# Pooled attention and a top-2 mixture of experts on one core: the unrolled expert part holds 1200 rows per expert instead of 1216

## The chip, the core and the metric

The kernel runs on one core of a Trainium2 chip. A core has TensorE (PE in the profile, with its weight loads as PEld), VectorE (DVE), ScalarE (ACT), GpSimd (POOL) and SyncE (SP). They share an on-chip memory (SBUF), and PE writes its products into PSUM, which DVE and ACT read. The metric is the device time of one execution in microseconds (us); lower is better.

## What is computed

Attention with keys and values averaged over eight positions gives 4608 token rows `x` of 512. A noisy gate then sends each row to the two best of eight experts. Each expert is a two-layer product, and the rows come back weighted:

```python
top2 = np.argpartition(-noisy_logits, 2, axis=1)[:, :2]
top2_w = np.exp(top2_l - top2_l.max(-1, keepdims=True)); top2_w /= top2_w.sum(-1, keepdims=True) + 1e-09
for e in range(E):                       # E = 8, x: 4608 x 512, w1[e]: 512 x 1024, w2[e]: 1024 x 512
    for k in range(2):
        mask = top2[:, k] == e
        h = np.maximum(x[mask] @ w1[e], 0.0)
        out[mask] += top2_w[mask, k, None] * (h @ w2[e])
```

On average an expert gets 4608 x 2 / 8 = 1152 rows. The reference evaluated on its inputs gives the eight experts 1135, 1130, 1185, 1163, 1193, 1176, 1107 and 1127 rows. In the kernel the list of expert 0 has two gaps (its second half begins at row 512 at the earliest, and a later part at row 896), so that it ends at row 1174.

## The kernel before

The first part (to about 184 us of the trace) is attention: products, exponentials, and at its end the gate. Each token's two (row, weight) records are scattered into `rec_dram`, a list for each expert with room for `ER` rows. The list is filled ahead with an index out of range (`BIG`), so that unused places are gathered from a harmless row and never written.

The second part is the experts, one after the other, unrolled. The first `CAP` = 1216 places of each list are cut into tiles of 128 places, `t` = 0 to 9, of which tile 9 has 64. The tiles form three groups: tiles 0 to 3 (512 columns), tiles 4 to 6 (384) and tiles 7 to 9 (128 + 128 + 64 = 320). Expert 0 takes them in the order (0-3), (4-6), (7-9), the other seven in the order (0-3), (7-9), (4-6). For each group:

- `gather` (L703) fetches rows of `x` by indirect DMAs, four for a tile (two for tile 9). They are issued by POOL, and so are all other indirect DMAs.
- `split` (L917) turns each tile by a DVE transpose (`xt`) and cuts it into a high part `xh` (ACT, L939) and a low part `xl` (DVE, L939).
- `stage1` (L956) makes the first product in eight blocks `f` of 128 hidden columns. A block is 12 matmuls (four depth blocks, and the three products high-high, low-high, high-low) into a PSUM tile `ph`, of which there are three. ACT takes the block out as `hh` (L973) and DVE as `hl` (L974). Every second block (every block for tiles 0-3) a piece of later weights is converted too (L484, L485). Its staging buffers `wst` are refilled by SP.
- `stage2` (L1023) makes the second product. For tiles 0-3 and 4-6 it takes 24 matmuls of 512 columns for each tile into a PSUM tile `py` (three buffers). `finish` (L1003) multiplies by the token's weight, adds what `out` held (`pv`, gathered by POOL at L992) and scatters it (L1014).
- For tiles 7-9 the second product is turned the other way: four PSUM tiles `py` (`mb` = 0 to 3), each 24 matmuls with the tokens as columns (L1043). DVE transposes each into `yt` (L1048). Ten slices of 32 tokens are then multiplied and added (L1054) to what ten gathers (L1031) brought into the buffer `pv4`, and scattered (L1057). Tile 3 uses the same buffer `pv4` for its own rows, so the ten gathers wait until the scatter of tile 3 has landed.

After the eight experts a loop (L1210) takes any further rows, 128 at a time. Its count is worked out on the chip from `CAP`, and each turn loads its expert's weights anew.

A scheduler orders the instructions of each engine when the program is built. Each engine works through its own list in order, and waits between engines are semaphores that the tile framework sets. The framework takes two accesses to one PSUM bank as dependent even where they touch different columns.

Of the kernel before, what the change touches and what calls it, by code (L numbers as in the profile page):

```python
# [20 lines left out]
def kernel(  # L21
# [12 lines left out]
    nc = tc.nc  # L34
# [4 lines left out]
    P = 128  # L39
# [8 lines left out]
    NCH = 9  # L48
    EARLY = 4 * P
    EARLY2 = 7 * P  # L50
    SECT = ((0, 4, P), (4, 3, P), (7, 2, P), (9, 1, 64))
    CAP = 1216
    OV_T = -(-(NTOK - CAP) // P)
    ER = CAP + OV_T * P
    XT0 = NTOK // 2
    BIG = float(1 << 20)
# [574 lines left out]
    def load_recs(e0, e1, s0, s1, early=False):  # L631
        ne = e1 - e0
        t0, t1 = SECT[s0][0], SECT[s1 - 1][0] + SECT[s1 - 1][1]
        nt = t1 - t0
        nm = f"{e0}_{e1}_{t0}"
        V = nc.vector
        raw = rp.tile([P, ne, nt, 2], I32, name=f"raw{nm}")
        if s1 == len(SECT):
            V.memset(raw[64:, :, nt - 1, 0:1], int(BIG))
            V.memset(raw[64:, :, nt - 1, 1:2], 0)  # L640
        src = rec_dram.rearrange("(e r) c -> e (r c)", e=E)
        for ts, n, np_ in SECT[s0:s1]:
            o = ts * P * 2
            with nullcontext() if early else tc.issue_after(wld[1, 1, 0]):
                ld = (nc.gpsimd if RE >> (0 if early else 1 if e0 == 0 else 2) & 1 else nc.sync).dma_start(raw[:np_, :, ts - t0:ts - t0 + n].rearrange("p e t c -> p e (t c)"),
                                   src[e0:e1, o:o + np_ * n * 2].rearrange("e (p x) -> p e x", p=np_))
            genl[0] = ld.ins
            if early:
                tc.add_to_no_dep_group("rec_load0", ld.ins)

        def tl(w, dt=F32):
            return rp.tile([P, ne, nt], dt, name=f"{w}{nm}")

        w = ne * nt

        def spread(src, nm_):
            px = mone(f"{nm_}{nm}")
            for r in range(4):
                nc.tensor.matmul(px[:, r * w:(r + 1) * w], sel[:, r].rearrange("p u j -> p (u j)"),
                                 src.rearrange("p e t -> p (e t)"), start=True, stop=True)  # L660
            return px[:, :4 * w].rearrange("p (r e t) -> p r e t", r=4, e=ne)

        def late():
            xf = tl("xf")
            nc.gpsimd.tensor_copy(xf, raw[:, :, :, 0])
            wf = tl("wf")
            nc.gpsimd.tensor_copy(wf, raw.bitcast(F32)[:, :, :, 1])
            o = rp.tile([P, 4, ne, nt], I32, name=f"o{nm}")
            V.tensor_scalar(o, spread(xf, "px"), 4.0, qcol, op0=OP.mult, op1=OP.add)
            w4 = rp.tile([P, 4, ne, 3], F32, name=f"w4{nm}")  # L670
            V.tensor_copy(w4, spread(wf, "pw")[:, :, :, 7 - t0:10 - t0])
            x = rp.tile([P, 4, ne, nt], I32, name=f"x{nm}")
            V.tensor_single_scalar(x, o, float(4 * NTOK - 1), op=OP.min)
            for e in range(E):
                for t in range(7, 10):
                    oi4[e, t] = o[:, :, e, t:t + 1]
                    wc4[e, t] = w4[:, :, e, t - 7:t - 6]
                if e:
                    for t in range(10):
                        xi[e, t] = x[:, :, e, t:t + 1]  # L680

        if e1 == 1:
            x = tl("x", I32)
            nc.gpsimd.tensor_single_scalar(x, raw[:, :, :, 0], float((XT0 if t1 <= 4 else NTOK) - 1), op=OP.min)
        else:
            x = rp.tile([P, 3], I32, name=f"x{nm}_0")
            nc.gpsimd.tensor_single_scalar(x, raw[:, 0, 7:10, 0], float(NTOK - 1), op=OP.min)
            for t in range(7, 10):
                xi[0, t] = x[:, t - 7:t - 6]
        for e in range(0 if e1 == 1 else 1, e1):  # L690
            for t in range(t0, t1):
                i = (e - e0, t - t0)
                if e1 == 1:
                    xi[e, t] = x[:, i[0], i[1]:i[1] + 1]
                tokc[e, t] = raw[:, i[0], i[1], 0:1]
                wcol[e, t] = raw.bitcast(F32)[:, i[0], i[1], 1:2]
        return late
# [105 lines left out]
    for b in range(2, B):  # L803
        c = 9 * ((b - 2) // 2) + (0 if b % 2 == 0 else 4)
# [7 lines left out]
    for b in range(1, B):  # L812
        c = 9 * (b // 2) + (0 if b % 2 == 0 else 4)
# [96 lines left out]
    def w2s(e, hl, f):  # L910
        return W[e, 2 + f // 4][:, hl, (f % 4) * DM:(f % 4 + 1) * DM]
# [39 lines left out]
    pv4 = mp.tile([P, 10, P], F32, name="pv4")  # L951

    def cols(grp):
        return 320 if grp[1] == 7 else grp[2] * P

    def stage1(grp, hook=None):  # L956
        e, t0, nt = grp
# [65 lines left out]
    def stage2(grp, mid, hook=None):  # L1023
        e, t0, nt = grp
        hs = HT.pop(grp)
        n = cols(grp)
        if t0 == 7:
            yt = mp.tile([P, 10, NDB, 32], F32, tag="yt", name=f"yt{e}")
            if e:
                for i in range(10):  # L1030
                    g = nc.gpsimd.indirect_dma_start(  # L1031
                        out=pv4[:, i], out_offset=None, in_=out4,
                        in_offset=bass.IndirectOffsetOnAxis(ap=oi4[e, t0 + i // 4][:, i % 4], axis=0),
                        bounds_check=4 * NTOK - 1, oob_is_err=False)
                    tc.declare_no_dep(g.ins, group=f"out{e}", reason="rows of other tokens")
                    tc.add_to_no_dep_group(f"out{e}", g.ins)
            mid()
            for mb in range(NDB):
                py = mps.tile([P, DM], F32, tag="py", name=f"py{e}_{t0}_{mb}", bufs=3)
                i = 0  # L1040
                for f in range(NFB):
                    for a, b in PASSES:
                        nc.tensor.matmul(  # L1043
                            py[:, :n],
                            w2s(e, b, f)[:, mb * P:(mb + 1) * P],
                            hs[f][a][:, :n], start=(i == 0), stop=(i == 3 * NFB - 1))
                        i += 1
                nc.vector.transpose(yt[:, :, mb], py[:, :n].rearrange("p (c j) -> p c j", j=32))  # L1048
            r4 = pv4
            for i in range(10):  # L1050
                y = yt[:, i].rearrange("p m j -> p (m j)")
                wc = wc4[e, t0 + i // 4][:, i % 4]
                if e:
                    nc.vector.scalar_tensor_tensor(r4[:, i], y, wc, pv4[:, i], op0=OP.mult, op1=OP.add)  # L1054
                else:
                    nc.vector.tensor_scalar(r4[:, i], y, wc, None, op0=OP.mult)
                s = nc.gpsimd.indirect_dma_start(  # L1057
                    out=out4, out_offset=bass.IndirectOffsetOnAxis(ap=oi4[e, t0 + i // 4][:, i % 4], axis=0),
                    in_=r4[:, i], in_offset=None, bounds_check=4 * NTOK - 1, oob_is_err=False)
                for gr in (f"out{e}", f"outb{e}"):  # L1060
                    tc.declare_no_dep(s.ins, group=gr, reason="rows of other tokens")
                tc.add_to_no_dep_group(f"out{e}", s.ins)
            return
        pvs = [prev(e, t, P) for t in range(t0, t0 + nt)]
        mid()
        for t in range(t0, t0 + nt):
            cs = slice((t - t0) * P, (t - t0 + 1) * P)
            py = mps.tile([P, DM], F32, tag="py", name=f"py{e}_{t}", bufs=3)
            i = 0
            for f in range(NFB):  # L1070
                for a, b in PASSES:
                    lastm[0] = nc.tensor.matmul(py, hs[f][a][:, cs], w2s(e, b, f),  # L1072
                                                start=(i == 0), stop=(i == 3 * NFB - 1))
                    i += 1
            finish(e, t, P, py, pvs.pop(0))
            if hook:
                hook(t - t0)

    def mone(name):
        return mps.tile([P, 512], F32, tag="xp", name=name, bufs=2)  # L1080
# [63 lines left out]
    for i, g in enumerate(groups):  # L1144
# [18 lines left out]
        if i == 0:  # L1163
            lates.append(load_recs(0, E, 0, 4))
            fetch(groups[2])
            with tc.issue_after(hli[g, NFB - 1].ins):
# [3 lines left out]
    thr = rp.tile([P, OV_T], F32, name="thr")  # L1170
    nc.gpsimd.iota(thr, pattern=[[P, OV_T]], base=CAP, channel_multiplier=0,
                   allow_small_or_imprecise_dtypes=True)
# [19 lines left out]
    nc.vector.tensor_sub(sg[:, 1:2], prow, red[:, 1:2])  # L1192
    nc.vector.tensor_scalar(sg[:, 0:1], red[:, 0:1], float(ER), float(CAP), op0=OP.mult, op1=OP.add)
    nc.vector.scalar_tensor_tensor(sg[:, 0:1], sg[:, 1:2], float(P), sg[:, 0:1], op0=OP.mult, op1=OP.add)
# [15 lines left out]
    with tc.For_i(0, totr, 1) as it:  # L1210
# [34 lines left out]
        py = ops.tile([P, DM], F32, name="opy")  # L1245
# [35 lines left out]
```

## Time and profile before

| | us |
|---|---|
| median of 3 runs | 1040.61 |
| range of the runs | 1039.6 to 1043.3 |
| the profiled execution, its own time | 1040.2 |
| its span, first to last instruction | 1038.1 |
| PE busy | 1015.6 |
| POOL busy | 636.0 |
| DVE busy | 561.3 |
| ACT busy | 339.5 |

The span is 2.1 us shorter than the time of the execution, which also covers what lies around the first and the last instruction. Busy times are sums over a span with two different parts, so a stage is read from its own stretch of the trace. In a row of the trace the bracket gives how long the engine stood idle before the instruction and what released it. A matmul's duration in a row covers its whole way through the array; matmuls overlap, so how fast they follow each other is read from their starts or from the length of a stage.

### The profile page before, as it was taken

What the parts mean: (1) busy time and instruction counts of PE and PEld (TensorE: products, weight loads), DVE (VectorE), ACT (ScalarE), POOL (GpSimd) and SP (SyncE); (2) the same over time, 40 slices, a digit from 0 to 9 for tenths busy, and PEclk for the clock granted to TensorE, in tenths of its full rate; (3) what the DMA queues carried; (4) which work ended last, traced back from release to release, by engine and by line L of the source; (5) the groups of instructions that cost most, each with busy time, mean ns of one, the idle gap of its engine ahead of it and who ended that gap; (6) DMA issues with size and microseconds to landing.
All of it is one profiled execution on the core that took longest, in us unless ns stands there. A gap on an engine that the chain in (4) does not pass through costs nothing. (4 is left out here: it accounts for less than half of the span.)

```text
span 1038.1 us, 16083 instructions
## 1 busy us (share of the span) xinstructions
PE 1015.6 (98%) x5896; PEld 917.2 (88%) x5896; DVE 561.3 (54%) x1289; ACT 339.5 (33%) x857; POOL 636.0 (61%) x662
## 2 busy tenths in 40 slices
PE   7999999999999989999999999999999999999996
PEld 6999898889988988899889988998899889988995
DVE  6799897923654545454545454446444644554331
ACT  5588788402321232123212221222222222222110
POOL 4004555565777677767767775777577757773541
PEclk9799999999999999999999999999999999999999
DMA  9997985754333423442444234424342443232200
GB/s 322 363 339 243 241 272 185 183 157 124 102 93 116 135 67 114 131 132 69 124 126 140 69 115 128 135 70 120 118 130 75 117 122 120 80 91 87 69 20 31
DMA packets 77028, 142.13 MB, mean 137 GB/s; under 512 B 24501, under 2 KB 32778, under 8 KB 76948
## 3 DMA queue, kind: packets, MB, share of 16 engines
q1 hardware_dynamic: 48628, 78.33, 24.7%
q0 software_dynamic: 28320, 62.77, 20.2%
q8 instruction: 47, 0.77, 0.3%
q14 instruction: 33, 0.27, 0.1%
HBM read 103.78 MB, written 39.17 MB: 138 GB/s over the span
## 5 line engine op out<-in xcount | busy, mean ns | idle before, releaser
L968 PE MATMUL ph<-xh,w 128*128 128x384 f32 (+2 forms) x1536 | 404.3, 344 | 3.4 <-DVE hl L974 2.7
L714 POOL DMA_INDIRECT xg<-x_dram,x x266 | 260.6, 980 | 91.5 <-issue 66.1
L968 PEld LDWEIGHTS ph<-xh,w 128*128 128x128 f32 x1536 | 274.5, 188 | 24.1 <-DVE hl L974 3.0
L973 ACT ACTIVATE hh<-ph 128x512 fp32r<-128x512 f32 (+2 forms) x192 | 97.8, 509 | 552.2 <-PE ph L968 552.2
L1072 PE MATMUL py<-w,hh 128*128 128x512 f32 x896 | 276.5, 390 | 0.0
L968 PE MATMUL ph<-xl,w 128*128 128x320 f32 (+2 forms) x768 | 263.8, 344 | 0.0
L974 DVE SCALAR_TENSOR_TENSOR hl<-ph,hh 128x512 fp32r<-128x512 f32 (+2 forms) x192 | 111.1, 579 | 218.5 <-ACT hh L973 218.4
L1072 PEld LDWEIGHTS py<-w,hh 128*128 128x128 f32 x896 | 167.8, 188 | 34.2
L1072 PE MATMUL py<-w,hl 128*128 128x512 f32 x448 | 174.5, 390 | 0.0
L968 PEld LDWEIGHTS ph<-xl,w 128*128 128x128 f32 x768 | 144.2, 188 | 10.2
L1010 DVE SCALAR_TENSOR_TENSOR pv<-py,raw,pv 128x128 f32<-128x128 f32 x196 | 54.9, 342 | 130.9 <-PE py L1072 122.7
L1043 PE MATMUL py<-hh,w 128*128 128x320 f32 x512 | 112.8, 309 | 0.0
L1057 POOL DMA_INDIRECT out_dram<-pv,o x80 | 83.7, 1046 | 36.1 <-issue 14.3
L1072 PEld LDWEIGHTS py<-w,hl 128*128 128x128 f32 x448 | 84.1, 188 | 17.5
L1031 POOL DMA_INDIRECT pv<-out_dram,o x70 | 73.7, 1053 | 39.4 <-DMA out_dram<-pv,raw 20.2
L614 POOL DMA_INDIRECT rec_dram<-rec,pos x72 | 75.7, 1051 | 29.2 <-issue 19.8
L1014 POOL DMA_INDIRECT out_dram<-pv,raw x56 | 58.6, 1047 | 51.1 <-DVE pv L1010 31.7
L485 DVE TENSOR_TENSOR w<-wst,w 128x512 fp32r<-128x512 f32 x128 | 87.4, 686 | 0.9 <-ACT w L484 0.5
L1043 PEld LDWEIGHTS py<-hh,w 128*128 128x128 f32 x512 | 85.6, 188 | 0.0
L1043 PE MATMUL py<-hl,w 128*128 128x320 f32 x256 | 79.1, 309 | 0.0
L484 ACT CAST w<-wst 128x512 fp32r<-128x512 f32 x128 | 77.2, 615 | 3.3 <-PE ph L968 2.9
L934 DVE STREAM_TRANSPOSE xt<-xg 128x512 f32<-128x512 f32 (+1 forms) x70 | 70.8, 1034 | 6.9 <-DMA xg<-x_dram,x 6.5
(158 smaller groups left out, 990.8 us busy)
## 6 DMA issues: line engine op xcount, KB each, us to landing
wst<-in_moe_w_dram SPq DMA_DIRECT2D x64, 512.0 KB, 3.7
v<-in_v_dram SPq DMA_DIRECT2D x23, 512.0 KB, 10.1
k<-in_k_dram SPq DMA_DIRECT2D x7, 1280.0 KB, 12.0
q<-in_q_dram SPq DMA_DIRECT2D x7, 1024.0 KB, 11.7
x_dram<-xr POOLq DMA_DIRECT2D x12, 512.0 KB, 10.4
out_dram<-zt SPq DMA_DIRECT2D x6, 768.0 KB, 17.2
out_dram<-lg SPq DMA_DIRECT2D x6, 768.0 KB, 14.1
xg<-x_dram,x POOLq DMA_INDIRECT x276, 2.6
```

Source lines behind the costliest of these rows:

```text
L484: nc.scalar.copy(hv, sv)
L485: nc.vector.tensor_sub(lv, sv, hv.bitcast(F32))
L614: s = nc.gpsimd.indirect_dma_start(out=rec_dram[:, :], out_offset=bass.IndirectOffsetOnAxis(ap=pos[:, i, c:c + 1], axis=0), in_=rec[:, c, ...
L714: nc.gpsimd.indirect_dma_start(out=xg[:, r * P:(r + 1) * P], out_offset=None, in_=x4, in_offset=bass.IndirectOffsetOnAxis(ap=xi[e, t][:, r ...
L934: nc.vector.transpose(xt[:, :nr], xg[:, :nr * P].rearrange("p (r i b) -> p r b i", i=32, b=NDB))
L968: nc.tensor.matmul(ph[:, :n], w1s(e, a, db, f), xs[b][:, db, :n], start=(i == 0), stop=(i == 3 * NDB - 1))
L973: ra = nc.scalar.activation(hh[:, :n], ph[:, :n], AF.Relu)
L974: rd = hli[grp, f] = nc.vector.scalar_tensor_tensor(hl[:, :n], ph[:, :n], 0.0, hh[:, :n].bitcast(F32), op0=OP.max, op1=OP.subtract)
L1031: g = nc.gpsimd.indirect_dma_start(out=pv4[:, i], out_offset=None, in_=out4, in_offset=bass.IndirectOffsetOnAxis(ap=oi4[e, t0 + i // 4][:, ...
L1043: nc.tensor.matmul(py[:, :n], w2s(e, b, f)[:, mb * P:(mb + 1) * P], hs[f][a][:, :n], start=(i == 0), stop=(i == 3 * NFB - 1))
L1057: s = nc.gpsimd.indirect_dma_start(out=out4, out_offset=bass.IndirectOffsetOnAxis(ap=oi4[e, t0 + i // 4][:, i % 4], axis=0), in_=r4[:, i], ...
L1072: lastm[0] = nc.tensor.matmul(py, hs[f][a][:, cs], w2s(e, b, f), start=(i == 0), stop=(i == 3 * NFB - 1))
```

## The change

`CAP` becomes 1200, so tile 9 has 48 places and the last group has 304 columns. `cols` gives both products of that group 304. The rest of the group stays as it was: ten slices of 32 tokens are gathered, turned, multiplied and scattered. Since the transposes of the second product (now L1050) still read 320 columns of `py`, a memset on DVE (L1041) sets the 16 columns behind the product to zero first, once for each of the four tiles of an expert. The places 48 to 127 of tile 9 in the record tile `raw` hold `BIG`; a memset over whole columns writes that before the 48 records are loaded over it. The loop for further rows begins at row 1200, and the lists are 16 rows shorter.

```diff
-    SECT = ((0, 4, P), (4, 3, P), (7, 2, P), (9, 1, 64))
-    CAP = 1216
+    CAP = 1200
+    LAST = CAP - 9 * P
+    SECT = ((0, 4, P), (4, 3, P), (7, 2, P), (9, 1, LAST))
...
-            V.memset(raw[64:, :, nt - 1, 0:1], int(BIG))
-            V.memset(raw[64:, :, nt - 1, 1:2], 0)
+            V.memset(raw[:, :, nt - 1, 0:1], int(BIG))
+            V.memset(raw[:, :, nt - 1, 1:2], 0)
...
     def cols(grp):
-        return 320 if grp[1] == 7 else grp[2] * P
+        return 2 * P + LAST if grp[1] == 7 else grp[2] * P
...
                 py = mps.tile([P, DM], F32, tag="py", name=f"py{e}_{t0}_{mb}", bufs=3)
+                nc.vector.memset(py[:, n:320], 0.0)
...
-                nc.vector.transpose(yt[:, :, mb], py[:, :n].rearrange("p (c j) -> p c j", j=32))
+                nc.vector.transpose(yt[:, :, mb], py[:, :320].rearrange("p (c j) -> p c j", j=32))
```

Apart from the 32 memsets, the lists of the engines hold the same instructions, some of them with other widths; in one place, in expert 7, two DVE neighbours change places. The memsets stand at two kinds of places. The first is DVE's list where expert 1 passes from tiles 0-3 to tiles 7-9 (`pv_...` with `py_0` to `py_3` are the multiplies of `finish`, `hl_7_0` is the first block of tiles 7-9). Before:

```order
L1010 SCALAR_TENSOR_TENSOR pv_2677<-py_1_4013,raw_8_0_3136,pv_2677 128x128 x4
L1010 SCALAR_TENSOR_TENSOR pv_2678<-py_2_4045,raw_8_0_3136,pv_2678 128x128 x4
L1010 SCALAR_TENSOR_TENSOR pv_2679<-py_3_4077,raw_8_0_3136,pv_2679 128x128 x4
L974 SCALAR_TENSOR_TENSOR hl_7_0_4123<-ph_7_0_4109,hh_7_0_4122 128x320
L974 SCALAR_TENSOR_TENSOR hl_7_1_4140<-ph_7_1_4126,hh_7_1_4139 128x320
```

And now, at the same place of DVE's list:

```order
L1011 SCALAR_TENSOR_TENSOR pv_2677<-py_1_4017,raw_8_0_3136,pv_2677 128x128 x4
L1041 MEMSET py_7_0_4327 128x16
L1011 SCALAR_TENSOR_TENSOR pv_2678<-py_2_4049,raw_8_0_3136,pv_2678 128x128 x4
L1041 MEMSET py_7_1_4354 128x16
L1011 SCALAR_TENSOR_TENSOR pv_2679<-py_3_4081,raw_8_0_3136,pv_2679 128x128 x4
L1041 MEMSET py_7_2_4381 128x16
L975 SCALAR_TENSOR_TENSOR hl_7_0_4127<-ph_7_0_4113,hh_7_0_4126 128x304
```

Three of the four memsets of the expert stand a whole first product ahead of the matmuls that need them. The second place is DVE's list during the second product of tiles 7-9 of expert 1 (`yt` are the transposes of `py`, `xl_4` the low parts of tiles 4-6, `xt_0` and `xt_1` tiles of the next expert). Before:

```order
L934 STREAM_TRANSPOSE xt_6_4268<-xg_6_3976 128x512
L934 STREAM_TRANSPOSE xt_0_4618<-xg_0_4303 128x512
L1048 STREAM_TRANSPOSE yt_4272<-py_7_0_4323 128x10x32
L939 TENSOR_TENSOR xl_4_4259<-xt_6_4268,xh_4_4258 128x4x128
L934 STREAM_TRANSPOSE xt_1_4622<-xg_1_4308 128x512
L1048 STREAM_TRANSPOSE yt_4272<-py_7_1_4349 128x10x32
```

And now:

```order
L935 STREAM_TRANSPOSE xt_6_4272<-xg_6_3980 128x512
L935 STREAM_TRANSPOSE xt_0_4626<-xg_0_4307 128x512
L1050 STREAM_TRANSPOSE yt_4276<-py_7_0_4327 128x10x32
L940 TENSOR_TENSOR xl_4_4263<-xt_6_4272,xh_4_4262 128x4x128
L1041 MEMSET py_7_3_4408 128x16
L935 STREAM_TRANSPOSE xt_1_4630<-xg_1_4312 128x512
L1050 STREAM_TRANSPOSE yt_4276<-py_7_1_4354 128x10x32
```

The memset for `mb` = 3 stands two rows behind the transpose that frees its buffer. The first matmul of `mb` = 3 waited for that transpose before, and waits for the memset now.

## Rows read from the trace of the kernel before

**Rows 1.** The page: busy time, share and instructions of each engine.

```profile
PE 1015.6 (98%) x5896; PEld 917.2 (88%) x5896; DVE 561.3 (54%) x1289; ACT 339.5 (33%) x857; POOL 636.0 (61%) x662
```

**Rows 2.** Stages of expert 4: stretch, length, busy (instructions) by engine, clock, DMA.

```profile
core 0: us, PE busy (x) PEld busy (x) DVE busy (x) ACT busy (x) POOL busy (x), PEclk, DMA share, GB/s
611.42:633.18 21.76, 21.76 (x98) 18.02 (x96) 9.56 (x17) 6.73 (x12) 13.36 (x14) 1.00 0.51 157
...
654.94:669.01 14.07, 14.07 (x97) 14.07 (x96) 6.65 (x14) 4.58 (x10) 9.52 (x10) 1.00 0.51 162
669.01:683.09 14.08, 14.08 (x98) 14.08 (x97) 7.49 (x11) 2.61 (x5) 10.72 (x12) 1.00 0.31 86
683.09:699.74 16.65, 16.65 (x99) 16.65 (x98) 9.01 (x21) 5.82 (x12) 12.95 (x13) 1.00 0.26 84
```

**Rows 3.** PE in time, first product of tiles 4-6, expert 1: start, duration, idle.

```profile
372.14 0.34 PE L968 MATMUL ph<-xh,w 128*128 128x384 f32 x1
...
375.16 0.44 PE L968 MATMUL ph<-xh,w 128*128 128x384 f32 x1 [2.69 <-DVE hl L974]
```

**Rows 4.** DVE in time at the same place.

```profile
374.29 0.35 DVE L1054 SCALAR_TENSOR_TENSOR pv<-yt,w,pv 128x128 f32<-128x128 f32 x1 [1.05 <-DMA pv<-out_dram,o]
374.56 1.01 DVE L974 SCALAR_TENSOR_TENSOR hl<-ph,hh 128x384 fp32r<-128x384 f32 x2
```

**Rows 5.** POOL in time, from the record load to the last of the ten gathers.

```profile
247.81 0.70 POOL L687 TENSOR_SCALAR x<-raw 128x3 int32<-128x3 int32 x1 [6.79 <-DMA raw<-rec_dram]
...
326.46 1.04 POOL L992 DMA_INDIRECT pv<-out_dram,raw  x1 [2.15 <-issue]
...
355.12 1.02 POOL L1014 DMA_INDIRECT out_dram<-pv,raw  x1 [0.30 <-DVE xl L939]
360.32 1.01 POOL L1031 DMA_INDIRECT pv<-out_dram,o  x1 [4.18 <-DMA out_dram<-pv,raw]
...
372.04 1.11 POOL L1031 DMA_INDIRECT pv<-out_dram,o  x1 [0.30 <-issue]
```

**Rows 6.** DVE and SP in time, just ahead of that scatter.

```profile
353.22 0.69 DVE L485 TENSOR_TENSOR w<-wst,w 128x512 fp32r<-128x512 f32 x1
...
353.94 0.38 SPq L463 DMA_DIRECT2D wst<-in_moe_w_dram  x1
```

**Rows 7.** POOL in time at the same place of expert 5.

```profile
764.43 1.52 POOL L1014 DMA_INDIRECT out_dram<-pv,raw  x1 [0.31 <-DVE hl L974]
767.94 1.53 POOL L1031 DMA_INDIRECT pv<-out_dram,o  x1 [1.99 <-DMA out_dram<-pv,raw]
```

**Rows 8.** Stretches with other clocks or a full DMA, columns as in Rows 2.

```profile
26.00:39.60 13.60, 13.29 (x81) 12.14 (x80) 9.12 (x18) 5.64 (x21) 0.61 (x1) 0.50 1.00 334
356.00:358.00 2.00, 2.00 (x16) 2.00 (x14) 2.00 (x4) 0.62 (x1) 0.13 (x1) 1.00 1.00 385
372.50:375.10 2.60, 0.00 (x0) 0.00 (x0) 1.16 (x4) 0.49 (x1) 1.99 (x3) 1.00 0.01 0
1030.30:1032.90 2.60, 0.00 (x0) 0.00 (x0) 1.13 (x4) 0.00 (x0) 0.98 (x1) 1.00 0.03 6
1032.90:1038.00 5.10, 0.00 (x0) 0.00 (x0) 0.00 (x0) 0.00 (x0) 0.00 (x0) 0.50 0.13 53
```

**Rows 9.** DVE in time, second product of tiles 7-9, expert 1.

```profile
357.46 0.65 DVE L939 TENSOR_TENSOR xl<-xt,xh 128x512 fp32r<-128x512 f32 x1
```

**Rows 10.** The widest small memset of DVE.

```profile
L174 DVE MEMSET mbz<- 128x40 uint32 x1 | 0.1, 92 | 0.8 <-PEq L1267 0.8
```

**Rows 11.** DVE in time, end of tiles 7-9, expert 2.

```profile
473.93 0.52 DVE L1048 STREAM_TRANSPOSE yt<-py 128x320 f32<-128x320 f32 x1 [3.00 <-PE py L1043]
...
477.12 0.55 DVE L974 SCALAR_TENSOR_TENSOR hl<-ph,hh 128x384 fp32r<-128x384 f32 x1
```

**Rows 12.** Weight loads of PE in the second product of tiles 7-9.

```profile
L1043 PEld LDWEIGHTS py<-hh,w 128*128 128x128 f32 x512 | 85.6, 188 | 0.0
```

**Rows 13.** The page: weight loads by SP: count, size, us to landing.

```profile
wst<-in_moe_w_dram SPq DMA_DIRECT2D x64, 512.0 KB, 3.7
```

## The prediction

> **What bounds the kernel now.** I read the page's busy times first: PE is busy 98% of the span, the next engine, POOL, 61% [rows 1]. A busy PE alone says little, so I took one expert stage by stage. In every stage of expert 4 PE's busy time is as long as the stage [rows 2]. Each stage holds 96 matmuls (24 for each of four tiles, or 12 for each of eight blocks), as the counts of its weight loads show. So the distance from one matmul to the next is 21.76 / 96 = 226.7 ns at 512 columns, 16.65 / 96 = 173.4 ns at 384 and 14.07 / 96 = 146.6 ns at 320. The differences are 53.3 ns for 128 columns and 26.8 ns for 64, both 0.417 ns a column, which is one column per cycle at 2.4 GHz, the clock granted there. What is left, 13.3 ns, is the same at all three widths.
>
> Then I looked for places where PE waits. There is one of more than 2 us: 2.69 us at 375.16, in the first product of tiles 4-6 of expert 1 [rows 3]. PE has made three blocks there, all `ph` buffers are full, and DVE has not taken out the first, because the multiplies of tiles 7-9 stand ahead of it. The last of those waits for a gather until 374.29, and the `hl` follows at 374.56 [rows 4]. That gather is the tenth of a row that POOL issues 1.3 us apart, from 360.32 to 372.04 [rows 5]. POOL is late there: from 247.81, where it got the records, to the tenth gather it stands idle for more than 0.31 us only twice, 2.15 us at 326.46 and 4.18 us at 360.32, and both times it waits for its own transfers to land [rows 5]. POOL's timetable up to this point is thus its own, not PE's.
>
> **The change, part by part.**
>
> *The narrower products.* Both products of tiles 7-9 go from 320 to 304 columns: 16 x 0.417 = 6.67 ns for each matmul, 96 matmuls a stage, two stages an expert, eight experts: 1536 x 6.67 ns = 10.24 us. It all lies on PE, the path that sets the end; each stage gives 0.64 us.
>
> *What is given back at the wait in expert 1.* Four of the sixteen stages (two of expert 0, two of expert 1) lie ahead of the wait, so PE arrives there 2.56 us earlier. If the tenth gather came when it does now, the wait would grow from 2.69 to 5.25 us and the 2.56 us were lost. But the 4.18 us before the first gather can shrink. That gather waits for the scatter of tile 3, issued at 355.12 [rows 5]. Just ahead of it, at 353.94, SP requests 512 KB of weights as soon as DVE has emptied a staging buffer at 353.22 + 0.69 [rows 6], and the DMA engines are full from 356 to 358 at 385 GB/s [rows 8]. In expert 5 the same wait is 1.99 us [rows 7], so at most 4.18 - 1.99 = 2.19 us can go. The weight request hangs on PE's pace in tiles 7-9, and moves ahead by 1.28 us (expert 0) + 0.64 us (the first product of expert 1) = 1.92 us. It then lands ahead of most of the scatter. I take 1.8 us off POOL's wait, near the full 2.19. The wait of PE becomes 2.69 + 2.56 - 1.8 = 3.45 us, and 0.76 us of the saving is given back (bounds 0.37 and 2.56).
>
> *The clock.* The granted clock stayed at its upper level, 2.4 GHz, through the 2.69 us wait; at the end of the run it stood at that level for 2.6 us after the last matmul and then fell to 1.2 GHz [rows 8]. A wait of 3.45 us is longer than both, so I expect the clock to fall in it. The matmuls behind it then start at half speed, and half of that stretch is lost. No row prices this for wide matmuls. From below it is nothing (no fall). From above there is the only stretch inside the run at 1.2 GHz, 13.6 us with transposes and narrow products on PE [rows 8]: 6.8 us. Behind the wait PE gets the 384-column stream that holds the upper level everywhere else, so I stay near the lower end, at a quarter of the upper one: 1.7 us. *The Trainium skill ("TensorE: Matmul & The Clock Gate", HAM oscillation) says that a pause in which PE waits for a transfer brings the clock to its lower level and that the next burst starts slow. By that rule the fall is certain; the trace bears out the fall after the end.*
>
> *The memsets.* 32 on DVE, for which the 92 ns of a 128x40 memset is the nearest row [rows 10]: 3 us in all. DVE is busy about half the time. The first three of an expert are queued before the first product of tiles 7-9 has begun, and their matmuls come 13 us later. The fourth makes PE wait for DVE, behind the third low part of tiles 4-6. In expert 1 this ends at 357.46 + 0.65 = 358.11 [rows 9]. PE gets to `mb` = 3 there at 360.15 in the new timing: the next stage began at 366.07 (372.14, the last of 36 matmuls, less 35 x 0.1734 [rows 3]), less 24 x 0.1466 for the last product, less 2.40 us saved by then. So 2.0 us of cover are left, and I cost the memsets at nothing. Queued behind the fourth on DVE are the next `xt` and the transposes of `py`, which have microseconds to spare.
>
> *The rest.* The record load now waits for two memsets at the start of the program: nothing. 16 columns less for ACT and DVE in 128 evictions, off the path: nothing. POOL and SP issue what they did, in the same order. The next place where POOL could be late is expert 2: its `hl` ends at 477.12 + 0.55 = 477.67 [rows 11], and PE needs it after three blocks of 12 x 0.1734, which is 473.73 + 6.24 = 479.97 (the stage begins 0.2 us before the transpose at 473.93). PE comes 1.28 us earlier against POOL, so 1.0 us is left and nothing is lost. Later POOL has more room. The loop for further rows runs in neither kernel: the longest list has 1193 rows.
>
> **Sum**, against the profiled execution (1040.2 us, 0.4 below the median of 1040.61): 1040.2 - 10.24 + 0.76 + 1.7 = 1032.4 us.
>
> **The rivals.**
>
> *The clock stays up.* All as above, without the 1.7: 1030.7 us. For it: the two waits that the trace shows differ by 0.1 us and came out differently, so length alone does not decide, and 3.45 us may shrink further.
>
> *POOL's wait doesn't shrink*, because the weights now collide with the scatter ahead of this one. The whole 2.56 us is given back: 1032.5 us, with the clock's 1.7 us 1034.2.
>
> *Narrower is not faster.* One weight load of PE lasts 188 ns [rows 12], more than the 146.6 ns from matmul to matmul, and in the two 320-column stages loads are busy throughout (14.07 of 14.07 us, against 18.02 of 21.76 at 512 [rows 2]). If the loads were the floor there, 304 columns would gain nothing: 1040.2 us. Against it: at 384 columns loads are busy throughout too (16.65 of 16.65), and still 64 columns fewer gave the full 0.417 ns a column. *The Trainium skill ("Perfetto Trace Analysis", Identifying the Most-Contended Engine) says to judge PE's headroom by the busy share of the weight loads, which speaks for this rival.*
>
> *The fourth memset comes late.* If DVE got to it 1 us after PE needs it, that would be 8 us in eight experts: 1040.4. It takes 3 us of delay on DVE.
>
> *Slower: the loop runs.* It decides from the first list with more than 1200 rows. One turn loads 4 MB of weights in the open: 8 x 512 KB at 3.7 us [rows 13] = 29.6 us one after the other, or 10.9 us at 385 GB/s. That gives 1043 to 1062 us. The lists leave 7 rows of margin, so only other data would do it.
>
> **How the numbers follow.** Chances: the forecast 0.48 (own range 1030.9 to 1036: the clock's price 0.2 to 5), the clock stays up 0.29, POOL's wait doesn't shrink 0.10, narrower is not faster 0.06, a late memset 0.04, the loop 0.03. The forecast is the likeliest, 1032.4. The range from 1029.9 to 1036 takes in the first three. A difference under 0.3%, 3.1 us, can't be told from none here. Faster by more: the first three and a little of the rest, 0.89; within: 0.07; slower: the loop and a memset later still, 0.04.
>
> **What would show it right or wrong.** In the new trace the 304-column stages last 96 x 0.140 = 13.44 us and the others as now. POOL's wait before the ten gathers of expert 1 is about 2.4 us, PE's wait behind it about 3.5, and the granted clock shows a stretch at 0.50 behind it. Experts 2 to 7 take 103.4 us each instead of 104.7. A 320-column pace, a wait of PE at `mb` = 3, a PE wait in expert 2, or instructions of the loop would make it wrong.

## The result, and the profile after

| | before | after |
|---|---|---|
| median, us | 1041.68 (4 runs) | 1032.03 (4 runs) |
| range, us | 1039.6 to 1043.3 | 1029.6 to 1033.71 |
| profiled execution, its span | 1040.2, 1038.1 | 1031.38, 1029.3 |

The changed kernel takes 0.9899 of the time, with a 95% interval from 0.9869 to 0.9929: 9.65 us less by the medians. 1032.4 was forecast, with a range from 1029.9 to 1036. The sum came out nearly right, but two of its terms did not. Both were too small, and they have opposite signs. The base helped too: the sum starts from one execution of 1040.2 us, 1.5 below the median of the kernel before in this table, so that 7.8 us of saving were forecast where 9.65 were measured.

First the page and four stages of expert 4 (stretch, length, busy time and instructions of PE, PEld, DVE, ACT and POOL, granted clock, DMA share, GB/s), to be held against [rows 1] and [rows 2]:

```profile
PE 1001.6 (97%) x5896; PEld 903.0 (88%) x5896; DVE 561.1 (55%) x1321; ACT 338.0 (33%) x857; POOL 634.7 (62%) x662
```

```profile
609.63:631.39 21.76, 21.76 (x97) 18.03 (x96) 9.56 (x17) 6.72 (x12) 14.99 (x16) 1.00 0.51 160
653.15:666.38 13.23, 13.23 (x97) 13.22 (x96) 6.63 (x15) 4.50 (x10) 8.86 (x9) 1.00 0.51 172
666.38:679.61 13.23, 13.23 (x99) 13.23 (x97) 7.37 (x12) 2.59 (x5) 10.18 (x11) 1.00 0.32 87
679.61:696.27 16.66, 16.66 (x98) 16.66 (x97) 8.97 (x21) 5.80 (x12) 12.98 (x13) 1.00 0.26 80
```

The 512- and 384-column stages are what they were. The 304-column stages last 13.23 us where 13.44 was forecast: one product every 13.23 / 96 = 137.8 ns instead of every 140.0. A stage gives 0.85 us, not 0.64, and sixteen give 13.6 us, not 10.24.

The next view is PE, DVE, SP and POOL in time, where PE waits in expert 1 (start, duration, engine, idle time ahead and what ended it), against [rows 3] to [rows 6]:

```profile
374.46 0.69 PE L969 MATMUL ph<-xh,w 128*128 128x384 f32 x1 [4.33 <-DVE hl L975]
```

```profile
373.58 0.35 DVE L1056 SCALAR_TENSOR_TENSOR pv<-yt,w,pv 128x128 f32<-128x128 f32 x1 [1.05 <-DMA pv<-out_dram,o]
373.85 1.01 DVE L975 SCALAR_TENSOR_TENSOR hl<-ph,hh 128x384 fp32r<-128x384 f32 x2
```

```profile
352.42 0.38 SPq L464 DMA_DIRECT2D wst<-in_moe_w_dram  x1
```

```profile
355.58 1.01 POOL L1015 DMA_INDIRECT out_dram<-pv,raw  x1 [0.30 <-issue]
359.36 1.01 POOL L1032 DMA_INDIRECT pv<-out_dram,o  x1 [2.76 <-DMA out_dram<-pv,raw]
...
371.33 1.12 POOL L1032 DMA_INDIRECT pv<-out_dram,o  x1 [0.30 <-issue]
```

The chain is the forecast one: scatter of tile 3, ten gathers, multiplies, `hl`, PE. POOL's wait for the scatter fell from 4.18 to 2.76 us. PE's wait grew from 2.69 to 4.33 us, where 3.45 was forecast. The clock fell in it, as the windows of that stage show (columns as above):

```profile
363.70:374.46 10.76, 6.43 (x39) 6.12 (x37) 4.41 (x13) 1.98 (x4) 8.32 (x9) 0.92 0.12 33
374.46:379.49 5.03, 5.03 (x16) 5.03 (x17) 1.68 (x4) 0.73 (x2) 3.81 (x5) 0.50 0.19 51
379.49:387.27 7.78, 7.78 (x46) 7.78 (x45) 3.31 (x6) 3.09 (x7) 5.95 (x7) 1.00 0.46 126
```

PE worked for 5.03 us at 0.50, the 1.2 GHz level, and 2.6 us of the stage went there: 23.57 us from 363.70 to 387.27, less 4.33 of waiting, less the 16.66 us that the stage takes in expert 4.

The whole difference of the two traces can be laid out by the starts of the stages. The experts begin 2.1 us earlier (182.21 against 184.27), but their first two stages take 2.9 us longer in this trace. In five further traces, those of the experiments without pauses below, they take the 45.6 us of before in three, 46.4 in one and 47.0 in one. Among the three is `filler_2`, whose stages up to there are those of the changed kernel, so I count this as spread and not as the change. From there to the waiting stage 3.2 us are saved, that stage takes 3.9 us more, the six later experts take 10.1 us less (618.2 against 628.2), and the end 0.3 less. Together that is 8.8 us, the difference of the spans. The change's own part is -3.2 + 3.9 - 10.1 = -9.4 us.

The memsets, as one group of the changed kernel (instructions, busy us, mean ns):

```profile
L1041 DVE MEMSET py<- 128x16 f32 x32 | 2.2, 72 | 1.8
```

No instruction of PE waited for one of them. One scatter of POOL did, for 3.1 us in expert 7. The two scatters ahead of it waited 3.1 us each for multiplies, so the memset only stands in the place of one, and PE did not feel it.

### The profile page after: what moved, and what is told of

Read it like the earlier page. It is cut to its first block, busy times and chain, and to the rows that moved or that the text cites. A ratio compares the mean times of both kernels' runs of the same rounds, so it can differ in the third digit from the quotient of the medians.

```text
span 1029.3 us, 16131 instructions
## 1 busy us (share of the span) xinstructions
PE 1001.6 (97%) x5896; PEld 903.0 (88%) x5896; DVE 561.1 (55%) x1321; ACT 338.0 (33%) x857; POOL 634.7 (62%) x662
## 5 line engine op out<-in xcount | busy, mean ns | idle before, releaser
L969 PE MATMUL ph<-xh,w 128*128 128x384 f32 (+2 forms) x1536 | 399.8, 342 | 5.5 <-DVE hl L975 4.8
L969 PE MATMUL ph<-xl,w 128*128 128x304 f32 (+2 forms) x768 | 263.2, 343 | 0.0
L1045 PE MATMUL py<-hh,w 128*128 128x304 f32 x512 | 106.0, 300 | 0.0
L1045 PEld LDWEIGHTS py<-hh,w 128*128 128x128 f32 x512 | 83.0, 188 | 0.0
L485 ACT CAST w<-wst 128x512 fp32r<-128x512 f32 x128 | 77.2, 614 | 7.5 <-DMA wst<-in_moe_w_dram 4.5
L1045 PE MATMUL py<-hl,w 128*128 128x304 f32 x256 | 76.5, 299 | 0.0
```

Source lines behind the costliest of these rows:

```text
L485: nc.scalar.copy(hv, sv)
L969: nc.tensor.matmul(ph[:, :n], w1s(e, a, db, f), xs[b][:, db, :n], start=(i == 0), stop=(i == 3 * NDB - 1))
L1045: nc.tensor.matmul(py[:, :n], w2s(e, b, f)[:, mb * P:(mb + 1) * P], hs[f][a][:, :n], start=(i == 0), stop=(i == 3 * NFB - 1))
```

## Experiments

In three of the sessions (that of `widths`, `narrow_from_2`, `narrow_0_1` and `filler`, that of `from_0_1_again` and `memset_only`, and that of `from_0_1_third`) every kernel, the one before included, took 1274 to 1343 us, with all engines standing still at many places for a reason that no row names, so that from these only stretches in which PE ran without a pause are used. There `narrow_from_2` came out at a ratio of 1.01 to the kernel before (1.0047 to 1.0154) and `filler` at 1.0074 (0.9984 to 1.0164). The kernels whose question was still open were run again under other names.

**How long a product of n columns takes.** `widths` gives tiles 7-9 another width in each expert and product:

```diff
+    WID = ((320, 304), (288, 272), (312, 296), (316, 308), (306, 298), (318, 302), (264, 256), (280, 240))
-    def cols(grp):
-        return 2 * P + LAST if grp[1] == 7 else grp[2] * P
+    def cols(grp, stage=0):
+        return WID[grp[0]][stage] if grp[1] == 7 else grp[2] * P
```

> The last group (tiles 7-9) of each expert gets two widths of its own, for the first and the second product: expert 0: 320, 304; 1: 288, 272; 2: 312, 296; 3: 316, 308; 4: 306, 298; 5: 318, 302; 6: 264, 256; 7: 280, 240. The lists fit into each. It asks why the matmuls at 304 columns follow each other every 137.8 ns and not every 140.0. Theory (a step): something at 320 columns and above costs some 2 ns a matmul, and below it the pace is columns x 0.417 ns + 11.1: 316 columns 142.8 ns, 312 141.1, 308 139.4, 304 137.8, 288 131.1, 272 124.4, 256 117.8, 240 111.1. Rival A (a straight line with a fixed part of 13.3 ns, and 304 is an oddity of its size, such as not being a multiple of 64): 312 143.3 ns, 288 133.3, 272 126.7, 256 120.0, 240 113.3, and only some sizes stand 2 ns below. Rival B (a cost that grows with the columns, 0.557 ns a column between 304 and 320): 312 142.2 ns, 288 128.9, 272 120, and so on down.

The means of the distances from one product to the next at the upper clock, worked out from the starts in the trace of `widths` (distances more than 13 ns off the median of their width left out), and what is left of each when n x 0.417 ns is taken off:

```
columns  240   256   264   272   280   288   296   298   302   304   306   312   316   318   320   384   512
ns     112.1 119.4 119.8 125.3 127.5 131.9 136.1 137.4 139.6 137.7 140.9 142.8 143.8 146.7 146.6 173.4 227.1
rest    12.1  12.7   9.8  12.0  10.9  11.9  12.8  13.2  13.7  11.1  13.4  12.8  12.2  14.2  13.3  13.4  13.8
```

(308 columns ran without a pause for too short a time.) Two windows show it too (columns as above): three tiles of 24 products at 304 columns in `widths`, and a stage of 96 products at 288 columns in `cap_1184`, which is described below (a window also counts the product that its edge cuts):

```profile
348.19:358.11 9.92, 9.92 (x73) 9.92 (x73) 7.96 (x13) 1.98 (x4) 5.51 (x6) 1.00 0.35 83
```

```profile
955.99:968.63 12.64, 12.64 (x97) 12.63 (x96) 4.41 (x12) 2.88 (x7) 7.23 (x8) 1.00 0.16 54
```

They give 9.92 / 72 = 137.8 ns and 12.64 / 96 = 131.7 ns. Neither the step nor the steeper line holds: on the whole the pace follows 0.417 ns a column plus a rest, as in the rival with the straight line, but the rest is not fixed. It is 13.3 to 13.8 ns at 320, 384 and 512 and lies between 9.8 and 14.2 elsewhere, with no order in the columns that I can name. The undisturbed traces give 304, 320, 384 and 512 columns the same means within 0.4 ns and, at 288, the 131.7 above; the other widths were seen in this one trace alone. At 320 nearly all distances are 146 or 147 ns; at 304 most lie between 133 and 142. So 304 is a good width: it is quicker than 302. Why is open. The floor by weight loads does not exist down to 240 columns: these loads last 188 ns [rows 12], and products follow each other every 112.

**The wait for tile 3's scatter.** `own_buffer` is the changed kernel with a buffer `pv3own` for tile 3. The ten gathers are then free of its scatter:

```diff
+    pv3 = mp.tile([P, DM], F32, name="pv3own")
...
-            pv = pv4[:, :4].rearrange("p i c -> p (i c)")
+            pv = pv3
...
-                    tc.declare_no_dep(g.ins, group=f"out{e}", reason="rows of other tokens")
+                    for gr in (f"out{e}", f"outb{e}"):
+                        tc.declare_no_dep(g.ins, group=gr, reason="rows of other tokens")
```

`own_buffer_1216` is the same edit in the kernel before. In both, a small tile of the attention part (`wrb`) moves to that part's own memory to make room.

> The changed kernel, with a buffer of its own for tile 3, so that the ten gathers of tiles 7-9 no longer wait for tile 3's scatter to land; POOL then issues the ten gathers further ahead in its list. Theory (POOL's wait for that scatter is what makes PE wait in expert 1): PE's wait of 4.3 us there goes, the clock stays at 1.00 behind it, and 4.3 + 2.5 us come off: about 1025 us. Rival (POOL is late by its own work, or the earlier gathers push back those of x and PE waits for them instead): PE waits as long at this or another place, 1030 us or more.

> The same buffer of its own for tile 3 in the kernel before (320 columns). Theory: its wait of 2.69 us goes, 1037 to 1038 us. With no wait in expert 1 in either, the difference from the changed kernel with this buffer is the pure price of the columns: 1536 matmuls x (146.6 - 137.7 ns) = 13.6 us. Rival (a part of the narrower stages' saving is lost elsewhere too): a difference of 10 us or less.

Measured in one session with a median of 1038.20 us for the kernel before (13 runs): `own_buffer` 1021.89 us, ratio 0.9832 (0.9787 to 0.9877); `own_buffer_1216` 1034.22 us, ratio 0.9955 (0.9921 to 0.9989). POOL in time of `own_buffer` shows the ten gathers right behind those of tiles 0-3, long ahead of tile 3's scatter:

```profile
328.80 1.00 POOL L994 DMA_INDIRECT pv3own<-out_dram,raw  x1 [0.30 <-issue]
330.11 1.00 POOL L1033 DMA_INDIRECT pv<-out_dram,o  x1 [0.30 <-issue]
...
341.82 1.00 POOL L1033 DMA_INDIRECT pv<-out_dram,o  x1 [0.30 <-issue]
343.12 1.40 POOL L715 DMA_INDIRECT xg<-x_dram,x  x1 [0.30 <-DVE hl L976]
...
367.61 1.07 POOL L1016 DMA_INDIRECT out_dram<-pv3own,raw  x1 [0.30 <-issue]
```

The stage in which PE used to wait, and all waits of PE from 205 us to its last product (engine, line, waited for: us, times, longest):

```profile
361.61:378.28 16.67, 16.67 (x98) 16.67 (x97) 8.97 (x21) 5.80 (x12) 12.90 (x13) 1.00 0.46 150
```

```profile
PE xp L929 <- DMA xg<-x_dram,x: 0.6, 1, 0.6
```

The stage takes 16.67 us instead of 23.57, at the upper clock throughout. The one wait left, 0.6 us, lies at 222.13, in expert 0; behind it PE waits for nothing up to its last product at 1012.80. From the second group of expert 0 to PE's last product the traces hold 784.1 us, against 791.1 in the changed kernel: the 4.33 and 2.6 us are both back. The rival, that PE would wait elsewhere, falls. Against `own_buffer_1216` (797.5 us) the same stretch shows the pure price of the columns: 13.3 us in sixteen stages, or 12.3 by the medians. By the traces this version beats both kernels. By the times it beats the kernel before, while its interval still touches that of the changed kernel (0.9869 to 0.9929).

**The clock.** `filler_2` puts 20 products that nobody reads into PE's wait:

```diff
+            if grp == (1, 4, 3) and f == 3:
+                fp = mps.tile([P, NDB * P], F32, tag="xp", name="fill", bufs=2)
+                for z in range(NFILL):
+                    nc.tensor.matmul(fp[:, :n], w1s(e, 0, 0, f), xs[0][:, 0, :n], start=True, stop=True)
```

> The changed kernel with 20 extra 384-column products, whose result nobody reads, ahead of the fourth block of the first product of tiles 4-6 of expert 1: 3.5 us of work inside PE's wait of 4.3 us. Theory (the half-speed stretch behind the wait comes from PE standing still): the block behind the wait begins when it did, PE's idle time there falls to about 0.9 us, the clock stays at 1.00, and the 2.5 us of the slow stretch come back: 2.5 us faster than the changed kernel. Rival (the clock falls there for another reason, or the extra products delay the next block): as fast as the changed kernel, with the slow stretch still there, or 1 to 3 us slower.

Its time is 1025.82 us (1022.3 to 1031.31), ratio 0.9888 (0.9833 to 0.9942): too wide to tell 2.5 us from the changed kernel's 0.9899. The trace does tell it. PE in time, and the stage:

```profile
363.56 3.63 PE L972 MATMUL fill<-xh,w 128*128 128x384 f32 x20
367.65 0.44 PE L974 MATMUL ph<-xh,w 128*128 128x384 f32 x1 [0.45 <-DVE hl L980]
```

```profile
357.30:378.18 20.88, 20.43 (x118) 20.11 (x117) 9.49 (x21) 5.80 (x12) 16.00 (x17) 1.00 0.27 70
```

The stage takes 20.88 us with all the extra products in it, 2.7 us less than in the changed kernel, at clock 1.00. The block behind the wait still begins when `hl` is done. So the slow stretch came from PE standing still.

**What the four narrow stages ahead of the wait are worth.** `from_2_again` has 304 columns only in experts 2 to 7:

```diff
-        return 2 * P + LAST if grp[1] == 7 else grp[2] * P
+        return (2 * P + LAST if grp[0] > 1 else 320) if grp[1] == 7 else grp[2] * P
```

> 304 columns only in experts 2 to 7; experts 0 and 1 keep 320, so PE and POOL come to the wait in expert 1 as in the kernel before. Theory (the four narrow stages ahead of the wait gain nothing, since the longer wait with its slow clock costs more than they give): the wait of PE in expert 1 stays at about 2.7 us, the clock stays at 1.00 behind it, and 12 stages x 0.85 us = 10.2 us come off: as fast as the changed kernel or up to 1 us faster. Rival (the four narrow stages do count): 3 us slower than the changed kernel.

It took 1028.68 us, ratio 0.9897 (0.9845 to 0.9948), the same as the changed kernel's ratio within the intervals. PE's wait is that of the kernel before, but the clock fell in it:

```profile
370.32 0.69 PE L969 MATMUL ph<-xh,w 128*128 128x384 f32 x1 [2.58 <-DVE hl L975]
```

```profile
361.33:370.29 8.96, 6.41 (x38) 6.09 (x36) 4.31 (x13) 1.98 (x4) 6.83 (x8) 0.97 0.11 27
370.29:376.51 6.22, 6.18 (x19) 6.19 (x20) 2.72 (x5) 1.00 (x2) 4.70 (x6) 0.50 0.21 55
376.51:383.69 7.18, 7.18 (x43) 7.18 (x42) 2.32 (x4) 2.83 (x6) 5.55 (x6) 1.00 0.43 128
```

The stage takes 22.36 us: 16.66, 2.58 of waiting and 3.1 lost to the clock. So a wait of 2.58 us brought the clock down here, and one of 2.69 us in the trace of before did not. The six later experts take 618.2 us, the 10.1 us less of twelve narrow stages. From the second group of expert 0 to PE's last product this trace holds 793.1 us, against 791.1 in the changed kernel. With the clock down in both, the four stages ahead of the wait thus brought 2.0 us: 3.2 us saved ahead of it, less 1.75 us of longer wait (4.33 against 2.58), plus 0.5 us that the clock took more here. That lies between the theory, nothing, and the rival, 3 us. The opposite kernel, 304 columns in experts 0 and 1 alone, should have shown this by itself:

> 304 columns only in experts 0 and 1, 320 in the others. Theory (what the four stages save, 4 x 0.85 = 3.4 us, goes for the most part into PE's wait in expert 1, and into a slow stretch of 2.5 us behind it if the clock falls there): within 2 us of the kernel before, on either side; PE's wait 4.2 us or more, and POOL's 57 issues from the first gather behind the record load to its wait at the pv gather 1.7 to 2.1 us shorter in sum than the 58.06 us of the kernel before. Rival (the saving of these stages stays): 3.4 us faster than the kernel before.

It ran three times, each in one of the disturbed sessions: ratios 1.0069 (0.9978 to 1.0159) as `narrow_0_1`, 0.9932 (0.9865 to 1.0) as `from_0_1_again` and 1.0008 (0.9971 to 1.0044) here. The theory asked for 0.998 to 1.002 and the rival for 0.9967. The last interval just leaves out the rival's 0.9967, but with waits all over the traces I take this to decide nothing.

**The memsets alone.** `memset_only` is the kernel before, plus one line:

```diff
                 py = mps.tile([P, DM], F32, tag="py", name=f"py{e}_{t0}_{mb}", bufs=3)
+                nc.vector.memset(py[:, 304:320], 0.0)
```

> The kernel before (320 columns, 1216 rows) with the 32 memsets on 16 columns of the second product's tiles, and nothing else. Theory (they hide on DVE): the time of the kernel before within 1 us, 32 memsets of 72 ns, no wait of PE for one, PE's wait in expert 1 still about 2.7 us. Rival (the fourth memset of an expert comes late, or the memsets push DVE's multiplies and POOL behind them): each expert 0.3 to 1 us longer than 104.7 us, 2 to 8 us in all.

1330.47 us against 1329.88 in its session, ratio 0.9966 (0.9879 to 1.0054): an effect of 8 us is excluded, one of 2 is not. The better evidence is the trace of the changed kernel: no instruction of PE waited for a memset, and PE is busy for all of the 13.23 us of a 304-column stage.

**The loop.** `cap_1184` holds 1184 rows (288 columns), so that two lists spill over:

```diff
-    CAP = 1200
+    CAP = 1184
```

> The unrolled part holds 1184 rows (last group 288 columns), so that the lists of experts 2 (1185 rows) and 4 (1193 rows) spill over and the loop runs twice; everything stays computed. It prices the rival in which the loop runs. Theory: the narrower stages take 96 x 131 ns = 12.6 us, and each turn of the loop costs between 10.9 us (4 MB of weights at the full DMA rate) and 29.6 us (eight loads one after the other), so the time is that of the changed kernel less about 10 us plus 22 to 59 us. Rival: the turns hide in the last expert's work or share their loads, and cost under 10 us together.

1093.96 us beside 1038.63 for the kernel before. SP's requests of the records at the head of each turn, and the length of the first turn:

```profile
1018.75 0.37 SPq L1217 DMA_DIRECT2D orec<-rec_dram  x1
...
1055.73 0.35 SPq L1217 DMA_DIRECT2D orec<-rec_dram  x1
```

```profile
1018.75:1055.73 36.98, 17.72 (x84) 13.17 (x84) 2.57 (x5) 2.22 (x8) 3.04 (x3) 0.73 0.34 121
```

A turn lasts 37.0 us, and PE is busy in half of it. From the end of the experts' last product to the end of the span the trace takes 77.3 us, against 7.5 in the changed kernel: 34.9 us more for each turn, none of it beside the experts. That is more than the upper bound of 29.6: that bound held only the weights, and a turn also runs its gathers, products and scatter.

The same trace shows the wait in expert 1 once more, with four stages of 288 columns ahead of it:

```profile
374.86 0.69 PE L969 MATMUL ph<-xh,w 128*128 128x384 f32 x1 [5.28 <-DVE hl L975]
```

PE comes earlier still and waits longer. The clock falls in this wait too (it stands at 0.50 from 374 to 378), and 1.9 us are lost to it (the stage takes 23.87 us, less 16.66 and 5.28).

## Why the prediction was right

*The narrower products: right in kind, too small.* 13.6 us instead of 10.24 by the length of the stages, 13.3 where it was measured alone. The step that failed is that "what is left, 13.3 ns, is the same at all three widths" was taken over to a fourth. 0.417 ns a column would have given 6.67 ns a product; it gave 8.9, because the rest is 11.1 ns at 304.

*The give-back at the wait: right place, too small.* The stage cost 3.9 us more, where 0.76 + 1.7 = 2.46 was forecast. Counted from the second group of expert 0, PE came 3.2 us earlier to its wait, not 2.56, and POOL issued the tenth gather 1.56 us earlier (371.33 less 230.69, against 372.04 less 229.84), not 1.8. So PE's wait grew by 1.64 us, not by 0.76. The clock took 2.6 us instead of 1.7. These two errors, 1.5 us together, and the 3.4 us of the first one partly cancel in the sum.

*POOL's wait shrinks because the weight request moves ahead: the mechanism holds, the size was luck.* It shrank by 1.42 us (forecast 1.8). Over the traces of before, after, `from_2_again` and `filler_2` there are 28 such waits. Where SP's request lies between 1.84 us ahead of the scatter and 0.76 us behind it, POOL waits 3.58 to 4.95 us (7 cases). Where it is 1.86 us or more behind, or far off, 1.97 to 3.21 (20 cases). The one case with the request 3.16 us ahead is the changed kernel's, with 2.76. The seven waits of `cap_1184` bear the mechanism out: requests 2.79 and 3.84 us ahead of the scatter go with 2.37 and 2.48 us, four about 1.2 us ahead with 3.60 to 5.83 us, and the one far off with 1.97. But in `filler_2`, with the same narrow stages ahead as in the changed kernel, the request lies only 1.84 us ahead and POOL waits 4.05 us, since the scatter itself came earlier. So the shift that the forecast counted on need not come.

*"POOL's timetable up to this point is thus its own, not PE's": wrong by some 2 us.* POOL's 57 issues from 249.19, the first gather behind the record load, to its wait at 326.46 [rows 5] take 58.06 us in the kernel before, in `from_2_again` and in `own_buffer_1216`, which all have 320 columns up to there. They take 55.94 us in the changed kernel, 56.34 in `filler_2`, 56.32 in `own_buffer` and 56.41 in `cap_1184`, which are narrower. As two groups of the trace show (the gathers of `x` in that stretch, before and after: count, busy us, mean ns), the single issue got shorter:

```profile
L714 POOL DMA_INDIRECT xg<-x_dram,x x38 | 38.7, 1019 | 11.6 <-issue 10.1 <-DMA xg<-x_dram,x 0.9 <-PE ph L968 0.3
```

```profile
L715 POOL DMA_INDIRECT xg<-x_dram,x x38 | 36.5, 962 | 11.6 <-issue 9.1 <-DMA xg<-x_dram,x 0.9 <-DVE w L486 0.6
```

Why is told in the last section. Without these 2 us, PE's wait would have grown further. (The forecast also put the 2.15 us at 326.46 down to a transfer of POOL's own; the row says `issue`, so it shows no transfer that POOL waited for there. No term of the sum rests on it.)

*The clock falls: it did, but the reason given was too sharp.* "A wait of 3.45 us is longer than both, so I expect the clock to fall in it" made it a matter of length. With a fall at 2.58 us and none at 2.69, length did not decide between those two; at 4.33 us and, in `cap_1184`, at 5.28 us it fell as well. The loss was 3.1, 2.6 and 1.9 us, so it did not grow with the wait, and 1.7 was near the lowest of the three. The rival in which the clock stays up was a fair one.

*The memsets, the evictions, expert 2: nothing, as costed.* A memset took 72 ns. The first product of tiles 4-6 in expert 2 lasts 16.66 us from 473.61 to 490.27: no wait. The loop didn't run.

*The rival "narrower is not faster" fell plainly*: products follow each other faster than the 188 ns of one weight load at every width from 240 to 384 columns. The Trainium skill ("Perfetto Trace Analysis", Identifying the Most-Contended Engine), which spoke for it, names the busy share of the loads as one of two measures of PE's headroom. In this trace that measure misleads: loads are busy for 13.23 of 13.23 us in the 304-column stage, and 16 to 64 columns less still shorten it.

## What to carry to other kernels

What is saved ahead of a wait is partly lost in it, and the wait can cost more than its own length by the clock behind it: find the waits first, ask what sets them, and remove that together with the change (here one more buffer was worth another 7 us). A pace that fits three widths exactly is no proof for a fourth, so the rest in such a sum deserves bounds. Errors of opposite sign, and a base below the median, made this forecast look better than its steps.

## What the runs showed of the hardware

*POOL's issue of an indirect DMA is held up by some operations of DVE.* POOL and DVE in time of the kernel before:

```profile
269.80 0.94 POOL L714 DMA_INDIRECT xg<-x_dram,x  x1 [0.30 <-issue]
271.05 1.41 POOL L714 DMA_INDIRECT xg<-x_dram,x  x1 [0.30 <-issue]
```

```profile
270.95 0.69 DVE L485 TENSOR_TENSOR w<-wst,w 128x512 fp32r<-128x512 f32 x1
```

All 11 of the 57 issues above that last over 1.1 us overlap a DVE operation with two inputs from SBUF: the conversion of weights (`w`, L485) or a low part (`xl`, L939). In the changed kernel only 3 last that long. Over all gathers of `x` behind 250 us in the kernel before, an issue takes 951 ns on average with DVE idle, 946 beside an `hl`, which reads one input from PSUM, and 1137 beside a conversion of weights alone (24 issues). What decides is which of the two starts first. Here the issue does, and it takes no longer than alone:

```profile
299.34 0.94 POOL L714 DMA_INDIRECT xg<-x_dram,x  x1 [0.31 <-issue]
```

```profile
299.45 0.68 DVE L485 TENSOR_TENSOR w<-wst,w 128x512 fp32r<-128x512 f32 x1
```

Of these gathers, 81 overlap a conversion of weights. The 49 that began ahead of it took 944 to 982 ns. The 32 that began while it ran took 945 to 1467 ns, the longer the more of it was left (60 to 647 ns). So the narrower stages shortened POOL's issues by moving DVE's conversions against them. The Trainium skill ("SBUF — State Buffer", SBUF: two separate sides) tells of a port pair that DVE and GpSimd lock against each other for as long as the one that starts first runs, also for a DVE operation with two SBUF inputs if the GpSimd operation reads SBUF. The rows agree where DVE starts first; that an issue reads SBUF, no row shows.

*The pace of products is not a straight line in the columns.* The rest above 0.417 ns a column ranges from 9.8 ns (264) to 14.2 (318), and 304 columns follow each other every 137.7 ns, 302 every 139.6.

*The same idle time of PE can bring the clock down or not*: 2.58 us did in one run, 2.69 us did not in another. Waits of 4.33 and 5.28 us did.
